# Attention on one Trainium2 core: score matmuls of a pair of heads in five runs, the last 64 keys over 128 rows, and row sums without VectorE

## The chip, the cores and the metric

The kernel runs on one core of a Trainium2 chip (trn2). The time is that of the device in microseconds (us), the median of three runs. Five engines work side by side: TensorE (PE in the profile; PEld is its weight load), VectorE (DVE), ScalarE (ACT), GpSimd (POOL) and SyncE (SP), which issues the transfers. Matmuls write PSUM, which VectorE and ScalarE read and empty into SBUF.

## The reference

Three layers follow each other; the change touches the first alone.

```python
def _attn_ref(q, k, v, f):                       # (4, 8, 576, 64), f (4, 8, 576)
    scores = scale * np.matmul(q, k.transpose(0, 1, 3, 2))
    cum = np.cumsum(np.log(np.clip(f, 0.0001, 1.0)), axis=-1)
    decay = cum[:, :, :, None] - cum[:, :, None, :]
    scores = np.where(causal, -1000000000.0, scores + decay)
    attn = np.exp(scores - np.max(scores, axis=-1, keepdims=True))
    attn = attn / (np.sum(attn, axis=-1, keepdims=True) + 1e-09)
    return np.matmul(attn, v)

def reference(...):
    x = _attn_ref(...)            # to (2304, 512)
    x = _moe_ref(x, ...)          # soft mixture of 8 experts, 4 slots each
    return _moe2_ref(x, ...)      # 4 dense experts
```

## The kernel before

**Pairs and steps.** The 32 heads are worked in 16 pairs (`pr`), four to a batch. The 576 queries of a head are cut into row blocks of 128, 128, 128, 128 and 64, and by causality row block `j` meets the first 128 (j + 1) keys (576 for the last). A pair has seven steps, each a row block of one head, and they run one after the other through all pairs as a counter `g`:

```python
STEPS = ((0, 1), (0, 3), (0, 2), (0, 4), (1, 1), (1, 3), (1, 2))   # (head of the pair, row block)
```

This document calls them step 0 to step 6. Steps 0 and 4 take row blocks 1 and 0 together (256 and 128 keys), steps 1 and 5 row block 3 (512 keys), steps 2 and 6 row block 2 (384 keys). Step 3 takes the last 64 rows of both heads at once, one head in PSUM rows 0 to 63 and one in 64 to 127, over 576 keys, in two PSUM tiles.

**What happens to a step.** `scores` makes the score matmuls of the step, in float32r, each product in two parts (L227 over 128 rows, L228 over 66; L212 for step 3). `soft` lets VectorE add the mask and take the row extreme (L198, into `p_j`), and ScalarE the exponential with its row sum (L202). Two steps later `transposes` turns `p_j` on TensorE (L261; L252 for row blocks 0 and 1) into one of two PSUM buffers of the tag `pt`, and a copy takes it to SBUF: to `pta` or `ptb` on VectorE (L170) or ScalarE (L168). The transposes of step 3 are copied half by ScalarE and half by VectorE ("the half copies", 128x256 elements each); those of steps 1 and 5 whole by VectorE (128x512), those of steps 2 and 6 by ScalarE (128x384). At step 4 the block of the last 64 rows against the last 64 keys is turned too (L254), and VectorE copies 64 rows of it into `ptb` for each head (L258).

**Products with the values.** A step behind a pair's last, `av_a` (L291) and `av_b` (L279) multiply `pta` and `ptb` with the values in plain float32, the two heads side by side as 64 columns of the array each. `av_b` comes in two stretches: key blocks 3, 4 and 0 ahead of the transposes of the next pair's step 0, and the rest of 0, 1 and 2 after its step 3 scores. Key block 4, the last 64 keys, uses 64 rows of weights where all others use 128. The values of that block lie in a tile of 128 rows whose upper 64 are zeros, and the columns of `p_4` behind 576 are set to zero once, at the start.

**Normalization and logits.** `rs` holds the row sums by row block and head. `nat` turns the pair's output back (L306) and VectorE scales it with the inverse sums (L312); `plog` makes the logits of the next layer (L325, L327) and VectorE multiplies them (L329), followed by a small one (L340) and by the copies of step 4's transposes.

**What sets the order.** TensorE runs in the order in which the code is written: in the loop over `g` first `scores(g)`, then the value products, then `transposes(g - 2)`, then `nat` and the logits. The order on VectorE, ScalarE, GpSimd and SP is made by the scheduler, and each of them works through its queue in order. Score tiles have four PSUM buffers. Steps 1 and 5 use the same `p_3`, so step 1's mask may be written only after the transposes of the pair before have read it.

Of the kernel before, what the change touches and what calls it, by code (L numbers as in the profile page):

```python
# [9 lines left out]
F32 = mybir.dt.float32  # L10
# [24 lines left out]
def soft_moe_kernel(tc, a, out):  # L35
    nc = tc.nc
    pe, dve, act, pool, sp = nc.tensor, nc.vector, nc.scalar, nc.gpsimd, nc.sync
# [10 lines left out]
    with ExitStack() as top:  # L48
# [42 lines left out]
        sm = pool_on(top, "right", "sm", 4)  # L91
# [109 lines left out]
            p = pt_in[j][:, 0:k0]  # L201
            act.activation(p, p, AF.Exp, bias=nm, scale=-1.0, accum_out=sums)  # L202

        def scores(g):
            pr, st = divmod(g, NS)
            hh, j = STEPS[st]
            h = 2 * pr + hh
            if j == 4:
                ts = [scq.tile([128, 512], F32, tag="sc", name=f"sc_{g}_{i}")[:, 0:384 - 192 * i] for i in range(2)]
                for t, k0, k1 in zip(ts, (0, 384), (384, 576)):  # L210
                    for q, k, kk, j, hx in ((qa, ka, 128, 0, 1), (qa, ka, 128, 0, 0), (qb, kb, 66, 1, 0), (qb, kb, 66, 1, 1)):
                        pe.matmul(t if hx else t[0:64], lhsT=qpad[j][0:kk] if hx else q[0][0:kk, 512:576],  # L212
                                  rhs=k[hx][0:kk, k0:k1], start=j == 0 and hx == 1,
                                  stop=j == 1 and hx == 1)
                r4 = sm.tile([128, 1], F32, tag="r4", bufs=1, name=f"r4_{pr}")
                soft(g, 4, ts, r4)
                for x in range(2):
                    i = (2 * pr + x) % 6
                    dve.tensor_copy(rs[0:64, 4, i:i + 1], r4[64 * x:64 * x + 64])
                return  # L220
            t, off = scq.tile([128, 512], F32, tag="sc", name=f"sc_{g}"), 0
            todo = []
            for c in (j,) if j > 1 else (1, 0):
                s0, n = START[c], START[c] + 128
                o = t[:, off:off + n]
                qs = slice(s0 + 64 * hh, n + 64 * hh)
                pe.matmul(o, lhsT=qa[hh][:, qs], rhs=ka[hh][:, 0:n], start=True, stop=False)  # L227
                pe.matmul(o, lhsT=qb[hh][0:66, qs], rhs=kb[hh][0:66, 0:n], start=False, stop=True)  # L228
                off += n
                todo.append((c, o))  # L230
            for c, o in todo:
                soft(g, c, (o,), rs[:, c, h % 6:h % 6 + 1])

        pta, ptb, cur = {}, {}, {}

# [3 lines left out]
        def transposes(g):  # L239
            pr, st = divmod(g, NS)  # L240
            hh, j = STEPS[st]
            h = 2 * pr + hh
            if g == NG - 1:
                t = scq.tile([128, 512], F32, tag="sc", name="pt_l").rearrange("p (i q) -> p i q", q=128)
            else:
                t = ptq.tile([128, 4, 128], F32, tag="pt", name=f"pt_{g}")
            if st in (1, 3):
                ptb[h + (st == 3)] = ptp.tile([128, 1280], F32, tag="ptb", bufs=2, name=f"ptb_{g}")
            if j == 1:
                pta[h] = ptp.tile([128, 384], F32, tag="pta", bufs=2, name=f"pta_{g}")  # L250
                for x, (c, i) in enumerate(((0, 0), (1, 0), (1, 1))):
                    pe.transpose(t[:, x, :], pt_in[c][:, 128 * i:128 * i + 128], ident)  # L252
                if st == 4:
                    pe.transpose(t[:, 3, :], pt_in[4][:, 512:640], ident)  # L254
                copy(act if g == NG - 3 else EV[1], pta[h], t[:, 0:3, :].rearrange("p a b -> p (a b)"))
                if st == 4:
                    for x in range(2):
                        dve.tensor_copy(ptb[h - 1 + x][0:64, 960:1024], t[0:64, 3, 64 * x:64 * x + 64])  # L258
                return
            for i in range(min(j + 1, 4)):  # L260
                pe.transpose(t[:, i, :], pt_in[j][:, 128 * i:128 * i + 128], ident)  # L261
            if j == 4:
                for x in range(2):
                    copy(EV[x + 4], blocks(ptb[h + x], 4)[:, :, 256:320], t[:, :, 64 * x:64 * x + 64])
                return
            c0 = 128 * (j - 2)
            copy(EV[j], blocks(ptb[h], j + 1)[:, :, c0:c0 + 128], t[:, 0:j + 1, :])
# [4 lines left out]
        def av_b(pr, i, q0, q1=320):  # L272
            if i == 3:
                av[pr] = tlq.tile([128, 512], F32, tag="av", name=f"avb_{pr}")
            t = av[pr]
            kk = 64 if i == 4 else 128
            b0 = 960 if i == 4 else 320 * i + q0
            for hh in range(2):
                pe.matmul(t[64 * hh:64 * hh + 64, q0:q1], lhsT=v_raw[pr][:kk, i, 64 * hh:64 * hh + 64],  # L279
                          rhs=ptb[2 * pr + hh][:kk, b0:b0 + q1 - q0], start=i == 3, stop=i == 2, skip_group_check=True)  # L280
            if i == 2:
                copy(EV[7], ot[pr][:, 256:576], t[:, 0:320])
                if pr + 1 < B * NP:
                    load_v(pr + 1)
# [179 lines left out]
                    csoft2(b)  # L464

        NG = NS * B * NP
        LAG = 2
        PS, PO = (3, 1)
        SPL = (3, 6)
# [25 lines left out]
        order = ExitStack()  # L495
        for g in range(NG + 4):
            pr, st = divmod(g, NS)
            if g < NG:
                scores(g)
                if g == GD:  # L500
                    for i in range(2):
                        decay(kb[i][96:128], slice(32 * i, 32 * i + 32))
                    first.close()
                    order.enter_context(tc.manual_schedule(engines={E.PE}))
                for h, s0 in ((1, 0),) if pr == 0 and st < 2 else ((2 * pr + 2, SPL[0]), (2 * pr + 3, SPL[1]), (2 * pr + 1, SPL[1] - 7)):
                    if h >= B * H:
                        continue
                    if st == s0:
                        split_a(h)
                        if 1 < h and h % 2 and h // 2 + 1 < B * NP:  # L510
                            load_q(h // 2 + 1)
                    if st == s0 + 1:
                        split_b(h)
                        if h + 2 < B * H:
                            load_k(h + 2)
                if pre and g >= GW and g % PS == PO:
                    pl = pre.pop(0)
                    if pl == "ring":
                        if not rt:
                            rt.append(ring.tile([128, 4096], F32, tag="w", name="ring_0"))  # L520
                        pl = rt[0][:, 4096 - 1024 * (len(pre) - NB + 1):4096 - 1024 * (len(pre) - NB)]
                    load_w(pl)
# [6 lines left out]
            before_tr(g - LAG + 2)  # L529
            if LAG <= g < NG + LAG:  # L530
                transposes(g - LAG)
            after_tr(g - LAG + 2)
        order.close()
        avs.close()
# [701 lines left out]
```

## Time and profile before

| what | us |
|---|---|
| median of three runs (675.5 to 676.67) | 676.22 |
| the profiled execution, its own time | 674.97 |
| its span, first to last instruction | 673.2 |
| TensorE busy in the span | 659.2 (98%) |
| VectorE busy | 493.3 (73%) |
| GpSimd busy | 419.4 (62%) |
| ScalarE busy | 342.6 (51%) |

A busy time is the union of an engine's instruction records. Matmuls are pipelined and their recorded ends are modelled, so a high share for TensorE is not TensorE at its peak, and a wait can lie under a record. The attention stage takes the first third of the span.

### The profile page before, as it was taken

Reading aid. Unit: us, or ns where it says so; the run is one execution under the profiler, and the core shown is the slowest. Engines: PE = TensorE matmul, PEld = TensorE weight load, DVE = VectorE, ACT = ScalarE, POOL = GpSimd, SP = SyncE. Lnnn points to the kernel's source line nnn. Section 1 sums busy time; section 2 is a strip of 40 time slices with the busy share of each in tenths; the row PEclk is TensorE's granted clock in tenths of the full one; section 3 lists DMA queues with packets and bytes.
Section 4 is the critical chain, followed back from the end, with each engine's and each line's share of the span. In section 5 each row is a group of like instructions: output and inputs, shape, how many; then the busy total and the mean of one; then the engine's idle time right before and its main releaser. Section 6 shows DMA issues by size and latency. Waiting matters only on the chain.

```text
span 673.2 us, 15292 instructions
## 1 busy us (share of the span) xinstructions
PE 659.2 (98%) x5634; PEld 581.6 (86%) x5634; DVE 493.3 (73%) x1358; ACT 342.6 (51%) x818; POOL 419.4 (62%) x392
## 2 busy tenths in 40 slices
PE   6999999999999998999999999999999999999997
PEld 4777777777777446999999999999999999999997
DVE  7888988988986004966778876778876767877774
ACT  5767767767764105543446443446443456543441
POOL 6667767767751046944589844589844589935443
PEclk7999999999999899999999999999999999999999
DMA  6587788733318893033000303000303000011111
GB/s 191 189 265 241 249 257 260 235 92 112 92 56 342 321 418 146 2 126 126 1 1 2 127 1 126 1 1 2 125 2 115 11 1 1 32 39 58 48 48 63
DMA packets 27138, 76.15 MB, mean 113 GB/s; under 512 B 3772, under 2 KB 4156, under 8 KB 27064
## 3 DMA queue, kind: packets, MB, share of 16 engines
q1 hardware_dynamic: 27064, 75.18, 32.5%
q8 instruction: 45, 0.74, 0.4%
q14 instruction: 29, 0.24, 0.1%
HBM read 70.31 MB, written 4.72 MB: 111 GB/s over the span
## 4 chain that ended last, share of the span: by engine, by line
PE 91%; DVE 4%; issue 2%; ACT 1%; DMA 0%; POOL 0%; DVEq 0%; ACTq 0%
PE R L1026 27%; PE Q L1026 13%; PE P L1026 6%; PE avb L279 6%; PE pt L261 6%; PE two L838 5%; PE d L1046 3%; PE sc L228 3%; PE sc L227 3%; PE sc L212 3%; PE pl L327 2%; PE two L734 2%; PE pt L252 2%; PE ava L291 2%; PE so_ps L758 2%
## 5 line engine op out<-in xcount | busy, mean ns | idle before, releaser
L904 POOL TENSOR_TENSOR s<-S,s 128x512 fp32r<-128x512 f32 x136 | 174.7, 1318 | 135.0 <-ACT s L900 135.0
L900 ACT CAST s<-S 128x512 fp32r<-128x512 f32 x136 | 75.0, 619 | 85.9 <-DVE S L896 55.0
L202 ACT ACTIVATE p<-p,nm 128x256 f32<-128x256 f32 (+2 forms) x144 | 83.4, 580 | 37.9 <-DVE nm L198 37.3
L1026 PE MATMUL R<-wh_T,s 128*128 128x256 f32 x544 | 86.6, 281 | 0.7 <-DVE acc L1009 0.7
L1009 DVE SCALAR_TENSOR_TENSOR acc<-R,dpn,acc 128x256 f32<-128x256 f32 x115 | 55.4, 482 | 37.5 <-PE R L1026 34.6
L870 ACT ACTIVATE a<-two 128x256 f32<-128x256 f32 x68 | 26.1, 383 | 96.9 <-PE two L838 96.5
L1026 PEld LDWEIGHTS R<-wh_T,s 128*128 128x128 f32 x544 | 73.5, 188 | 1.3 <-ACT a L879 1.2
L198 DVE CUSTOM_DVE_ANT_0 p<-sc,maskb 128x256 f32<-128x256 f32 (+2 forms) x144 | 66.2, 488 | 3.9 <-PE sc L212 0.9
L896 DVE SCALAR_TENSOR_TENSOR S<-two,S 128x256 f32<-128x256 f32 x136 | 57.0, 419 | 3.3 <-POOL s L904 0.9
L896 DVE SCALAR_TENSOR_TENSOR S<-two,a 128x256 f32<-128x256 f32 x136 | 56.2, 413 | 0.0
L179 POOL TENSOR_TENSOR opd<-raw,opd 64x576 fp32r<-64x576 f32 x30 | 44.3, 1477 | 11.1 <-ACT opd L168 9.8
L227 PE MATMUL sc<-opd 128*128 128x256 f32 (+3 forms) x128 | 47.4, 381 | 1.7 <-POOL opd L179 1.7
L261 PE MATMUL pt<-ident,p 128*128 128x128 f32 x285 | 47.3, 285 | 1.1 <-DVE ptb L170 0.3
L190 POOL TENSOR_TENSOR opd<-raw,opd 64x576 fp32r<-64x576 f32 x31 | 44.1, 1422 | 6.7 <-DVE opd L170 5.7
L838 PE MATMUL two<-c4t,gs 128*128 128x256 f32 x288 | 46.2, 283 | 0.3 <-ACT gs L168 0.3
L261 PEld LDWEIGHTS pt<-ident,p 128*128 128x128 f32 x285 | 31.4, 144 | 17.2 <-issue 14.6
L886 DVE SCALAR_TENSOR_TENSOR q<-two,q 128x512 fp32r<-128x512 f32 x68 | 46.2, 679 | 0.0
L1026 PE MATMUL R<-wh_T,q 128*128 128x256 f32 x272 | 43.8, 283 | 0.0
L279 PE MATMUL avb<-ptb,v 128*64 128x192 f32 (+3 forms) x384 | 43.8, 347 | 0.0
L180 POOL TENSOR_SCALAR opd<-raw 64x576 fp32r<-64x576 f32 x30 | 21.5, 717 | 35.2 <-PE sc L212 17.7
L1026 PE MATMUL Q<-wh_B,s 128*128 128x256 f32 x272 | 43.3, 281 | 0.0
L1026 PE MATMUL R<-wh_B,a 128*128 128x256 f32 x272 | 43.1, 280 | 0.0
(254 smaller groups left out, 1686.8 us busy)
## 6 DMA issues: line engine op xcount, KB each, us to landing
w<-in_w SPq DMA_DIRECT2D x50, 512.0 KB, 5.3
ring<-in_m SPq DMA_DIRECT2D x28, 512.0 KB, 6.6
raw<-in_k SPq DMA_DIRECT2D x64, 144.0 KB, 2.8
v<-in_v SPq DMA_DIRECT2D x16, 320.0 KB, 4.1
out<-acc SPq DMA_DIRECT2D x18, 256.0 KB, 2.0
raw<-in_q SPq DMA_DIRECT2D x15, 288.0 KB, 4.2
ring<-in_w SPq DMA_DIRECT2D x8, 512.0 KB, 4.5
w_opd<-in_w SPq DMA_DIRECT2D x4, 512.0 KB, 5.3
```

The lines of the kernel that those rows point to most:

```text
L198: dve.tensor_tensor_reduce(out=pt_in[j][:, k0:k0 + n], in0=sc, in1=maskb[:, m0:m0 + n], scale=-SCALE, scalar=nm, op0=ALU.add, op1=ALU.min, ...
L202: act.activation(p, p, AF.Exp, bias=nm, scale=-1.0, accum_out=sums)
L227: pe.matmul(o, lhsT=qa[hh][:, qs], rhs=ka[hh][:, 0:n], start=True, stop=False)
L261: pe.transpose(t[:, i, :], pt_in[j][:, 128 * i:128 * i + 128], ident)
L279: pe.matmul(t[64 * hh:64 * hh + 64, q0:q1], lhsT=v_raw[pr][:kk, i, 64 * hh:64 * hh + 64], rhs=ptb[2 * pr + hh][:kk, b0:b0 + q1 - q0], star ...
L838: pe.matmul(t[:, j, k], lhsT=gs[e][:, 128 * fc:128 * fc + 128], rhs=c4t[:, nb * BLK:nb * BLK + BLK])
L886: dve.scalar_tensor_tensor(o[:, 1], i, 0.0, f32(o[:, 0]), op0=ALU.max, op1=ALU.subtract)
L896: dve.scalar_tensor_tensor(sv[m, name][:, c], half[m, h][:, :, k, 128 * t:128 * t + 128], 0.0, other, op0=ALU.max, op1=op)
L900: act.copy(tile_of(m, name)[:, 0], sv[m, name])
L904: (eng or pool).tensor_tensor(o[:, 1], sv[m, name], f32(o[:, 0]), op=ALU.subtract)
L1009: dve.scalar_tensor_tensor(o, t, pcol, o, op0=ALU.mult, op1=ALU.add)
L1026: pe.matmul(t, lhsT=a[:, c, :], rhs=w[:, c, :], start=first and x == 0 and c == 0, stop=x == 2 and c == 3, skip_group_check=True)
```

## The change

The loop now takes its scores from a table: from the second pair on, the scores of step 1 are made together with those of step 0 and the scores of step 4 together with those of step 3, so that a pair has five runs of score matmuls. The mask and exponential of step 1 are held back until the transposes behind the run are written. The value products of the last 64 keys use all 128 rows, and the copies that feed them take 128 rows. The row sums of step 3 go straight into `rs` for both heads, and ScalarE copies the second head's 64 sums to the lower rows.

```diff
-        def scores(g):
+        def scores(g, hold=None):
...
-                r4 = sm.tile([128, 1], F32, tag="r4", bufs=1, name=f"r4_{pr}")
-                soft(g, 4, ts, r4)
-                for x in range(2):
-                    i = (2 * pr + x) % 6
-                    dve.tensor_copy(rs[0:64, 4, i:i + 1], r4[64 * x:64 * x + 64])
+                i, i2 = [(2 * pr + x) % 6 for x in range(2)]
+                soft(g, 4, ts, rs[:, 4, i:i + 1])
+                act.copy(rs[0:64, 4, i2:i2 + 1], rs[64:128, 4, i:i + 1])
                 return
...
             for c, o in todo:
-                soft(g, c, (o,), rs[:, c, h % 6:h % 6 + 1])
+                f = lambda c=c, o=o: soft(g, c, (o,), rs[:, c, h % 6:h % 6 + 1])
+                f() if hold is None else hold.append(f)
...
-                        dve.tensor_copy(ptb[h - 1 + x][0:64, 960:1024], t[0:64, 3, 64 * x:64 * x + 64])
+                        dve.tensor_copy(ptb[h - 1 + x][:, 960:1024], t[:, 3, 64 * x:64 * x + 64])
...
-            kk = 64 if i == 4 else 128
             b0 = 960 if i == 4 else 320 * i + q0
             for hh in range(2):
-                pe.matmul(t[64 * hh:64 * hh + 64, q0:q1], lhsT=v_raw[pr][:kk, i, 64 * hh:64 * hh + 64],
-                          rhs=ptb[2 * pr + hh][:kk, b0:b0 + q1 - q0], start=i == 3, stop=i == 2, skip_group_check=True)
+                pe.matmul(t[64 * hh:64 * hh + 64, q0:q1], lhsT=v_raw[pr][:, i, 64 * hh:64 * hh + 64],
+                          rhs=ptb[2 * pr + hh][:, b0:b0 + q1 - q0], start=i == 3, stop=i == 2, skip_group_check=True)
...
+        RUNS = {0: (0, 1), 2: (2,), 3: (3, 4), 5: (5,), 6: (6,)}
...
+            held = []
             if g < NG:
-                scores(g)
+                for x in RUNS.get(st, ()) if pr else (st,):
+                    scores(g - st + x, held if st == 0 and x else None)
...
             if LAG <= g < NG + LAG:
                 transposes(g - LAG)
+            for f in held:
+                f()
             after_tr(g - LAG + 2)
```

On TensorE, in the middle of a pair, behind the last score matmul of step 3 (`sc_1`), before:

```order
L212 MATMUL sc_1_1447<-opd_92 128x192
L279 MATMUL avb_1433<-ptb_1304,v_1301 64x128
L279 MATMUL avb_1433<-ptb_1339,v_1301 64x128
L279 MATMUL avb_1433<-ptb_1304,v_1301 64x320
L279 MATMUL avb_1433<-ptb_1339,v_1301 64x320
L279 MATMUL avb_1433<-ptb_1304,v_1301 64x320
L279 MATMUL avb_1433<-ptb_1339,v_1301 64x320
L261 MATMUL pt_1479<-ident,p_125 128x128 x4
L227 MATMUL sc_1486<-opd_92 128x256
L228 MATMUL sc_1486<-opd_92 128x256
L227 MATMUL sc_1486<-opd_92 128x128
L228 MATMUL sc_1486<-opd_92 128x128
```

and of the change:

```order
L212 MATMUL sc_1_1433<-opd_92 128x192
L225 MATMUL sc_1448<-opd_92 128x256
L226 MATMUL sc_1448<-opd_92 128x256
L225 MATMUL sc_1448<-opd_92 128x128
L226 MATMUL sc_1448<-opd_92 128x128
L277 MATMUL avb_1419<-ptb_1301,v_1298 64x128
L277 MATMUL avb_1419<-ptb_1325,v_1298 64x128
L277 MATMUL avb_1419<-ptb_1301,v_1298 64x320
L277 MATMUL avb_1419<-ptb_1325,v_1298 64x320
L277 MATMUL avb_1419<-ptb_1301,v_1298 64x320
L277 MATMUL avb_1419<-ptb_1325,v_1298 64x320
L260 MATMUL pt_1474<-ident,p_125 128x128 x4
```

The four score matmuls of step 4 moved ahead of the second stretch of value products and of the transposes of step 1.

On ScalarE, at the same place of the pair, from the exponential of step 3 (`p_126`) to that of step 5 (`p_125`); `p_123` and `p_122` are step 4's, `ot` the copy of the products. Before:

```order
L202 ACTIVATE p_126,r_7_1456<-p_126,nm_4_1_1459 128x576
L168 COPY ot<-avb_1433 128x320
L168 COPY ptb_1480<-pt_1501 128x3x128
L202 ACTIVATE p_123,rs<-p_123,nm_1_0_1491 128x256
L202 ACTIVATE p_122,rs<-p_122,nm_0_0_1494 128x128
L202 ACTIVATE p_125,rs<-p_125,nm_3_0_1509 128x512
L168 COPY ptb_1480<-pt_1512 128x4x64
```

and of the change:

```order
L202 ACTIVATE p_126,rs<-p_126,nm_4_1_1444 128x576
L202 ACTIVATE p_123,rs<-p_123,nm_1_0_1453 128x256
L217 COPY rs<-rs 64x1
L202 ACTIVATE p_122,rs<-p_122,nm_0_0_1456 128x128
L168 COPY ot<-avb_1419 128x320
L168 COPY ptb_1475<-pt_1485 128x3x128
L168 COPY ptb_1475<-pt_1496 128x4x64
L202 ACTIVATE p_125,rs<-p_125,nm_3_0_1493 128x512
```

Step 4's exponentials and the row-sum copy moved ahead of the three copies, and the half copy (128x4x64) ahead of step 5's exponential.

On VectorE, from there to the logit multiplication (`pln`); the rows L198 without an input read out a reduction. Before (the two row-sum copies of L219 stand right ahead of these rows):

```order
L170 COPY ptb_1480<-pt_1479 128x4x128
L198 ISA p_123,nm_1_0_1491<-sc_1486,maskb 128x256
L198 ISA nm_1_0_1491 128x1
L198 ISA p_122,nm_0_0_1494<-sc_1486,maskb 128x128
L198 ISA nm_0_0_1494 128x1
L198 ISA p_125,nm_3_0_1509<-sc_1506,maskb 128x512
L198 ISA nm_3_0_1509 128x1
L312 TENSOR_TENSOR xn_1182<-nat_1520,ri_1430 128x4x128
L198 ISA p_124,nm_2_0_1529<-sc_1526,maskb 128x384
L198 ISA nm_2_0_1529 128x1
L170 COPY ptb_1513<-pt_1512 128x4x64
L329 TENSOR_TENSOR pln_1546<-pl_1539,ri_1430 128x320
```

and of the change:

```order
L198 ISA p_123,nm_1_0_1453<-sc_1448,maskb 128x256
L198 ISA nm_1_0_1453 128x1
L198 ISA p_122,nm_0_0_1456<-sc_1448,maskb 128x128
L198 ISA nm_0_0_1456 128x1
L170 COPY ptb_1475<-pt_1474 128x4x128
L198 ISA p_125,nm_3_0_1493<-sc_1490,maskb 128x512
L198 ISA nm_3_0_1493 128x1
L170 COPY ptb_1497<-pt_1496 128x4x64
L310 TENSOR_TENSOR xn_1170<-nat_1504,ri_1416 128x4x128
L198 ISA p_124,nm_2_0_1513<-sc_1510,maskb 128x384
L198 ISA nm_2_0_1513 128x1
L327 TENSOR_TENSOR pln_1530<-pl_1523,ri_1416 128x320
```

Step 4's reductions moved ahead of the copy of step 1's transposes, and the half copy ahead of the normalization (`xn`) and of step 6's reduction (`p_124`).

## Rows read from the trace of the kernel before

**Rows 1.** Windows of two pairs: length; PE, PEld, DVE, ACT, POOL busy; clock; DMA.

```profile
109.08:120.72 11.64, 11.64 (x98) 9.16 (x97) 10.02 (x38) 8.39 (x26) 8.34 (x9) 1.00 0.75 237
147.14:159.05 11.91, 11.83 (x97) 9.17 (x97) 10.29 (x38) 8.42 (x26) 8.41 (x9) 1.00 0.35 105
```

**Rows 2.** TensorE's timeline in a pair: start us, length us, line, tiles, count.

```profile
147.84 1.23 PE L279 MATMUL avb<-ptb,v 128*64 128x192 f32 x12
149.01 0.55 PE L252 MATMUL pt<-ident,p 128*128 128x128 f32 x3
...
150.58 1.52 PE L279 MATMUL avb<-ptb,v 128*64 128x128 f32 x12
152.02 0.66 PE L261 MATMUL pt<-ident,p 128*128 128x128 f32 x4
...
153.52 0.39 PE L228 MATMUL sc<-opd 66*128 66x512 f32 x1
153.99 0.63 PE L261 MATMUL pt<-ident,p 128*128 128x128 f32 x4
```

**Rows 3.** VectorE's timeline in the same pair.

```profile
152.93 0.31 DVE L219 COPY rs<-r 64x1 f32<-64x1 f32 x2 [0.99 <-ACT p L202]
153.16 0.68 DVE L170 COPY ptb<-pt 128x512 f32<-128x512 f32 x1
...
155.09 0.69 DVE L312 TENSOR_TENSOR xn<-nat,ri 128x512 f32<-128x512 f32 x1
155.70 0.55 DVE L198 CUSTOM_DVE_ANT_0 p<-sc,maskb 128x384 f32<-128x384 f32 x1
...
156.32 0.42 DVE L170 COPY ptb<-pt 128x256 f32<-128x256 f32 x1
156.69 0.49 DVE L329 TENSOR_TENSOR pln<-pl,ri 128x320 f32<-128x320 f32 x1
...
157.76 0.33 DVE L258 COPY ptb<-pt 64x64 f32<-64x64 f32 x2
```

**Rows 4.** TensorE's timeline, the end of that pair.

```profile
157.10 0.23 PE L227 MATMUL sc<-opd 128*128 128x128 f32 x1
157.16 0.27 PE L228 MATMUL sc<-opd 66*128 66x128 f32 x1
157.28 0.62 PE L261 MATMUL pt<-ident,p 128*128 128x128 f32 x4
...
157.97 0.40 PE L228 MATMUL sc<-opd 66*128 66x512 f32 x1
158.25 0.52 PE L261 MATMUL pt<-ident,p 128*128 128x128 f32 x3
...
159.75 0.50 PE L279 MATMUL avb<-ptb,v 128*64 128x192 f32 x4
```

**Rows 5.** VectorE's timeline, the end of that pair.

```profile
158.95 0.67 DVE L170 COPY ptb<-pt 128x512 f32<-128x512 f32 x1
```

**Rows 6.** Weight loads over fifteen pairs, by form: busy us, mean ns | idle before.

```profile
L279 PEld LDWEIGHTS avb<-ptb,v 64*64 64x64 f32 x60 | 2.9, 131 | 4.2 <-issue 4.2
```

**Rows 7.** ScalarE's timeline in the same pair.

```profile
152.03 0.78 ACT L202 ACTIVATE p<-p,nm 128x576 f32<-128x576 f32 x1 [0.83 <-DVE nm L198]
...
152.81 0.41 ACT L168 COPY ot<-avb 128x320 f32<-128x320 f32 x1
153.54 0.48 ACT L168 COPY ptb<-pt 128x384 f32<-128x384 f32 x1 [0.33 <-PE pt L261]
154.34 0.51 ACT L202 ACTIVATE p<-p,nm 128x256 f32<-128x256 f32 x1 [0.32 <-DVE nm L198]
...
154.85 0.39 ACT L202 ACTIVATE p<-p,nm 128x128 f32<-128x128 f32 x1
...
155.94 0.35 ACT L168 COPY ptb<-pt 128x256 f32<-128x256 f32 x1
```

**Rows 8.** ScalarE's groups by line, the attention stage, its smallest operation.

```profile
L385 ACT ACTIVATE al<-mm,dm 128x1 f32<-128x1 f32 x3 | 0.9, 292 | 0.0
```

## Prediction, made before the change was run

> **What bounds the kernel now.** I first read the windows view, one window for each pair of heads in the attention stage, since every line of the change lies there. In a usual pair TensorE is busy for 11.83 of 11.91 us at a granted clock of 1.00, VectorE for 10.29, ScalarE for 8.42 and GpSimd for 8.41 [rows 1]. Twelve of the fifteen pairs whose runs are joined look like this; three, one behind each of the first three batches, are longer by that batch's own work on TensorE. So the stage goes at TensorE's pace. But its busy time hides waits, since a matmul's record runs on while the next one is held, so I read starts, not lengths, from its timeline.
>
> Three waits show there. First, the 512-column matmul at 153.52 is followed by the transposes of step 3 only at 153.99, 0.47 us later [rows 2]; an equal one later in the pair needs 0.28 (157.97 to 158.25) [rows 4], so 0.19 is lost. The transposes want one of two PSUM buffers, which VectorE empties with the copy at 153.16 (0.68 us) [rows 3]. That copy is late because VectorE stood idle for 0.99 us before the two row-sum copies of L219, which wait for ScalarE's exponential [rows 3]. Ten pairs show a loss like this (one of them half of it); in two, as in the 11.64 us pair [rows 1], it is absent.
>
> Second, near the end of the pair TensorE and VectorE arrive together. VectorE's two small copies end at 157.76 + 0.33 = 158.09 [rows 3], and the transposes that reuse their PSUM buffer start at 158.25 [rows 4]. The four-block copy at 158.95 ends at 159.62 [rows 5], and the value products that read it start at 159.75 [rows 4]. 0.15 us from the end of such a copy to TensorE's start is also what the first wait shows (153.84 to 153.99) [rows 2, 3], so VectorE, from the logit multiplication (156.69) [rows 3] on, is as much the bound here as TensorE.
>
> Third, the loads of 64-row weights for the last 64 keys were preceded by 4.2 us of idle time in fifteen pairs, 0.28 each [rows 6], with no other engine named.
>
> **The products over 128 rows.** The first stretch of value products runs from 147.84 to 149.01, 1.17 us for 192 + 64 + 192 = 448 columns a head; the second from 150.58 to 152.02, 1.44 us for 128 + 320 + 320 = 768 columns [rows 2]. At the second one's rate the first would take 1.44 x 448 / 768 = 0.84, so the detour into 64 rows and back costs 0.33 us. The idle time before the 64-row loads alone is 0.28 [rows 6], as the lower of two readings; nothing shows a 64-column product in the 128-row form. If it took as long as the next larger one there, 128 columns, it would cost 64 x 1.44 / 768 = 0.12 us more, and the gain would be 0.16 to 0.21. I take 0.30, between the two readings and without the floor, since the 64-column products that are there already leave no room for one: 0.28 of the 0.33 is the idle time before them. All 16 pairs have this once: 16 x 0.30 = 4.8 us, between 2.6 and 5.3. Behind the stretch TensorE goes on with transposes whose inputs are long ready, and with the scores of step 3. The VectorE copies from 64 to 128 rows keep their 64 columns and their time.
>
> **The joined score runs.** Leaving a score run for transposes costs 0.12 us after a 128-column matmul (157.16 to 157.28) against 0.06 to the next matmul inside the run (157.10 to 157.16) [rows 4]. So each join frees about 0.06 us, two in a pair, 15 x 0.12 = 1.8 us, if nothing waits. At the pair's start (step 1 with step 0) I take nothing: the same transposes still need the two small copies and the value products still need the four-block copy, and VectorE's order from the logit multiplication to both is unchanged, so TensorE only waits where it worked. At step 3 the value products and the transposes of step 1 move behind step 4's scores, about 0.4 us later, and with them VectorE's 0.68 us copy, so the 0.19 us loss stays although L219 is gone.
>
> The Trainium skill, TensorEngine Tiling (Array Packing), Key Properties, says that changing the tiling mode drains TensorE, while changing the tile within a mode does not. By that rule the joins would free nothing, since scores and transposes both use the whole array, and only the 64-row detour would gain; the 0.06 us above are a cost that the rule does not have. The sum is the same by either, because I count the joins at nothing.
>
> **The row sums, and the new order on ScalarE and VectorE.** VectorE loses two copies (0.31 us) and their 0.99 us wait [rows 3]. But softmax of step 4 now comes earlier on ScalarE, ahead of its PSUM copies. I follow its queue in the usual pair. The exponential of step 3 starts at 152.03 as before, and the next operation can start at 152.81 [rows 7]. Before, from there: product copy, block copy at 153.54, step 4's exponentials, step 5's, half copy at 155.94 to 156.29 [rows 7]. Now: exponential 0.51, row-sum copy, exponential 0.39, product copy 0.41, block copy 0.48, half copy 0.35 [rows 7]. For the row-sum copy I take 0.25: the smallest ScalarE operation here takes 0.29 with an exponential [rows 8]. The sum is 2.39, so the half copy ends at 155.20, 1.1 us earlier. The Trainium skill, ScalarE: Activation LUTs, Rules for kernel authors, budgets about 0.3 us for an ACTIVATE, which would add 0.05.
>
> On VectorE the matching half copy (156.32 now, 0.03 after ScalarE's ended [rows 3, 7]) moves ahead of the normalization at 155.09 and of step 6's reduction at 155.70. It would run from 155.23; 0.37 later (156.32 to 156.69) comes the normalization, which ran at 155.09 before, 0.61 later the reduction, and after its 0.55 the logit multiplication: 155.23 + 0.37 + 0.61 + 0.55 = 156.76, against 156.69 before [rows 3]. So what waits behind the half copy on VectorE is late, and the earlier ScalarE copy nearly pays it: I charge 0.04, as operations there start some hundredths before the one ahead ends (155.70 against 155.09 + 0.69) [rows 3]; in ten usual pairs that is 0.4 us. In the two pairs without the 0.19 loss TensorE was that much ahead, so these lose about 0.2 each, 0.4 us. The three long pairs have other TensorE work between; I count nothing there. Bounds: if the chain is 0.1 shorter, TensorE sets the time and 1 us comes back; if the row-sum copy takes twice as long, 12 x 0.25 = 3 us more.
>
> **Sum.** 4.8 - 0.4 - 0.4 = 4.0 us. The profiled execution took 674.97 us (span 673.2 and 1.77 around it), so 671.0 for one like it; it lay 1.25 us under the median of 676.22, so **672.2** beside that median. Its own range is 670.9 to 673.8.
>
> **The rivals.**
> *The waits go too.* If the four-block copy and ScalarE's chain are earlier than I work out, the 0.19 and the joins are gained: 10 x 0.19 + 1.8 + 0.8 = 4.5 us more, 667.7. For it: VectorE's 0.99 us idle time vanishes. Against: the ties at 158.25 and 159.75 [rows 4]. 0.15.
> *A smaller share of the detour.* The 64-column step has a floor, or the loss moves to the next VectorE copy: 16 x 0.16 to 0.21 less the 0.8, so a gain of 1.8 to 2.6, about 674. 0.15.
> *The change doesn't do what it says.* The gap before the 64-row loads comes from something else that stays, such as the wait for the value weights; then only the charges of 0.8 us are left against the long pairs' joins of 3 x 0.12: about 676.6. 0.10.
> *Slower: ScalarE's queue becomes the bound.* The row-sum copy reads another partition half of what the exponential's accumulator just wrote, and stands ahead of four operations on which VectorE's half copy, the normalization and the logits depend. From 0.25 + 4.0 / 12 = 0.58 us for it on, the gain is gone; at 0.8 us it is 12 x 0.22 = 2.6 us slower, 678.8. Against: no ScalarE operation as small as this takes that long [rows 8]. 0.08.
> The forecast keeps 0.52.
>
> **How the numbers follow.** A median of this kernel can tell about 0.2%, 1.35 us. The forecast, the first rival and the smaller share (0.52, 0.15 and most of 0.15) are faster than 674.87; the no-effect case and the rest are within; the ScalarE case is slower: 0.79, 0.13, 0.08. The range 668.3 to 675.0 holds the forecast, the smaller share, and the nearer half of the first rival.
>
> **What the profile after would show.** No 64-row weight loads and a first stretch of products of about 0.87 us show the first step right. Transposes of step 3 still about 0.47 us behind their 512-column matmul show that the copy holds them; 0.28 would show the first rival. The logit multiplication 4.6 to 4.8 us after step 3's exponential (152.03 to 156.69 now) [rows 3, 7] shows ScalarE's chain sized right; later than that, the last rival. Usual pairs should take about 11.65 us. The prediction is wrong if VectorE's chain from the logits to the value products gets shorter or longer, which I hold fixed.

## The result, and the profile after

The changed kernel takes 681.44 us (median of five runs, 679.45 to 683.12) against 676.22 for the kernel before: 1.0073 times as long, 95% interval 1.0048 to 1.0099. The forecast was 672.2, faster. The sign was wrong. The ratios of all runs here leave out two executions far above the rest, 713.19 us in e1 and 2203.93 us in e7, which the medians include.

The profiled execution has a span of 681.3 us, 8.1 more than before. It was the slowest of the five (683.12 us), and the one of the kernel before lay under its median, so the losses below are larger than the 5.2 us between the medians. To see where, I took the start of each pair's first value products (`ava`, L291 before, L289 after) from TensorE's timeline; the distance from one to the next is a "stretch", 15 in all, and stretch n runs from pair n - 1 to pair n (pairs 0 to 15).

| stretches | before, us | after, us | sum of the differences |
|---|---|---|---|
| 1, 2, 4, 11, 12 (usual) | 11.87 to 11.93 | 11.55 to 11.66 | -1.5 |
| 3, 7, 8 | 11.80, 11.90, 11.64 | 14.13, 12.65, 13.30 | +4.7 |
| 5, 9, 13 (with a batch's end, long) | 14.52 | 14.55, 14.29, 14.51 | -0.2 |
| 6, 10, 14 (behind it) | 11.89 to 11.90 | 12.86, 12.86, 12.87 | +2.9 |
| 15 (the last) | 10.29 | 11.23 | +0.9 |
| ahead of the first `ava`, behind the last | 23.26 and 465.5 | 24.00 and 466.1 | +1.3 |

So 8.5 us were lost in seven stretches, and the usual ones gained about 0.3 each, as forecast. The last row holds a difference of the clock: over the 24.75 us behind the last `ava` TensorE's granted clock was 0.93 before and 0.86 after. The windows view shows four of them (one late, one behind a batch's end, one usual, the last); it answers to [rows 1]:

```profile
47.14:61.27 14.13, 11.85 (x97) 9.28 (x96) 10.98 (x39) 9.22 (x29) 9.27 (x10) 1.00 0.74 223
87.48:100.34 12.86, 11.74 (x97) 9.33 (x96) 10.75 (x38) 8.63 (x27) 8.53 (x9) 1.00 0.74 249
153.44:165.04 11.60, 11.52 (x97) 9.29 (x96) 10.07 (x36) 8.54 (x27) 8.35 (x9) 1.00 0.36 107
204.02:215.25 11.23, 10.42 (x90) 8.21 (x89) 8.93 (x31) 7.09 (x23) 3.21 (x6) 1.00 0.70 264
```

TensorE is busy for 11.85 of 14.13 us in the late stretch and for 11.52 of 11.60 in the usual one, at the same granted clock: it waits. The view of waits names for what (us in total, times, longest), over the whole attention stage:

```profile
PE avb L277 <- DVE xn L338: 3.1, 3, 1.1
PE ava L289 <- DMA v<-in_v: 2.4, 3, 1.1
PE pt L251 <- ACT p L202: 1.4, 2, 0.9
PE nat L304 <- ACT ot L168: 1.3, 2, 0.7
PE pt L260 <- ACT p L202: 1.0, 2, 0.5
PE pt_l L260 <- ACT p L202: 0.7, 1, 0.7
```

None of these stood in the profile before. Each has a place of its own.

**The usual stretch came out as worked out.** TensorE's timeline from 153.44, which answers to [rows 2]:

```profile
153.44 0.87 PE L289 MATMUL ava<-pta,v 128*64 128x256 f32 x8
154.15 0.94 PE L277 MATMUL avb<-ptb,v 128*64 128x192 f32 x12
155.01 0.55 PE L251 MATMUL pt<-ident,p 128*128 128x128 f32 x3
...
159.51 0.40 PE L226 MATMUL sc<-opd 66*128 66x512 f32 x1
159.99 0.63 PE L260 MATMUL pt<-ident,p 128*128 128x128 f32 x4
```

The first stretch of products takes 0.86 us (154.15 to 155.01) for 1.17 before, and the transposes of step 3 are still 0.48 behind their matmul. ScalarE's queue, which answers to [rows 7]:

```profile
157.97 0.78 ACT L202 ACTIVATE p<-p,nm 128x576 f32<-128x576 f32 x1 [0.77 <-DVE nm L198]
...
159.15 0.19 ACT L202 ACTIVATION_READ_ACCUMULATOR p<-p,nm 128x1 f32 x1
159.36 0.19 ACT L217 COPY rs<-rs 64x1 f32<-64x1 f32 x1
159.58 0.40 ACT L202 ACTIVATE p<-p,nm 128x128 f32<-128x128 f32 x1
```

The row-sum copy takes the queue from 159.34 to 159.58, 0.24 us.

**The late stretches: the value load.** SyncE's queue in a usual stretch, first before, then after (start, length of the issue with its wait, line, tiles, count; `L133` is the value load of the next pair, `L128` half a key load). In the kernel before the stretch began at 147.14, in the changed one at 153.44:

```profile
151.63 0.47 SPq L128 DMA_DIRECT2D raw<-in_k  x1
152.20 0.54 SPq L133 DMA_DIRECT2D v<-in_v  x1
154.38 0.48 SPq L128 DMA_DIRECT2D raw<-in_k  x1
```

```profile
157.64 3.22 SPq L128 DMA_DIRECT2D raw<-in_k  x2
160.95 0.54 SPq L133 DMA_DIRECT2D v<-in_v  x1
161.58 0.63 SPq L185 DMA_DIRECT2D opd<-opd  x1
```

Before, the value load stood between the two key halves and started 5.1 us into the stretch, 6.85 ahead of the products that read it (159.05). After, it stands behind both, the second of which waits for GpSimd to finish with the buffer (2.2 us here), and starts 7.5 us into the stretch, 4.1 ahead of 165.04. Over stretches 1 to 12 it is 5.0 to 6.2 us into the stretch before and 7.5 to 10.2 after. In stretch 3 it comes too late; SyncE's queue, then TensorE:

```profile
48.90 1.13 SPq L128 DMA_DIRECT2D raw<-in_k  x2
...
56.31 0.49 SPq L128 DMA_DIRECT2D raw<-in_k  x1
57.33 1.03 SPq L133 DMA_DIRECT2D v<-in_v  x1
```

```profile
59.80 0.33 PE L226 MATMUL sc<-opd 66*128 66x384 f32 x1
61.27 0.87 PE L289 MATMUL ava<-pta,v 128*64 128x256 f32 x8 [1.15 <-DMA v<-in_v]
```

Its start at 57.33 is late for another transfer too: ScalarE's cast of the next query rows, ahead of step 3's exponential in its queue, had waited for them:

```profile
49.08 0.60 ACT L202 ACTIVATE p<-p,nm 128x384 f32<-128x384 f32 x1
...
52.59 0.67 ACT L168 CAST opd<-raw 64x576 fp32r<-64x576 f32 x1 [2.81 <-DMA raw<-in_q]
53.17 0.77 ACT L202 ACTIVATE p<-p,nm 128x576 f32<-128x576 f32 x1
```

That query load took 6.3 us from issue to landing; its counterpart before took 4.2. In the changed kernel the value load was issued 3.2 us ahead of it (43.05 and 46.27), before 6.3 us ahead (40.24 and 46.53).

**Behind a batch's end.** VectorE at the start of stretch 6, before:

```profile
84.66 0.47 DVE L329 TENSOR_TENSOR pln<-pl,ri 128x320 f32<-128x320 f32 x1
85.06 0.27 DVE L340 TENSOR_TENSOR xn<-pl,ri 64x128 f32<-64x128 f32 x1
85.25 0.67 DVE L198 CUSTOM_DVE_ANT_0 p<-sc,maskb 128x512 f32<-128x512 f32 x1
```

and VectorE and TensorE there in the changed kernel:

```profile
87.97 0.67 DVE L198 CUSTOM_DVE_ANT_0 p<-sc,maskb 128x512 f32<-128x512 f32 x1
...
88.58 0.48 DVE L327 TENSOR_TENSOR pln<-pl,ri 128x320 f32<-128x320 f32 x1
88.98 0.27 DVE L338 TENSOR_TENSOR xn<-pl,ri 64x128 f32<-64x128 f32 x1
```

```profile
87.48 0.87 PE L289 MATMUL ava<-pta,v 128*64 128x256 f32 x8
89.40 0.99 PE L277 MATMUL avb<-ptb,v 128*64 128x192 f32 x12 [1.05 <-DVE xn L338]
```

At the start of these three pairs TensorE also makes the logit products of the batch's last pair. Joined, step 1's scores stand ahead of them, and the held reduction of step 1 (87.97) stands ahead of the logit multiplication (88.58), where before it stood behind it (84.66, then 85.25). `avb` takes the PSUM buffer that the small operation behind it frees (88.98 + 0.27), and waits 1.05 us.

**The last stretch.** The last pair's turned row blocks of step 6 wait 0.74 us for their exponential, which stands behind a ScalarE copy of step 4's transposes (213.63) that itself waits for TensorE:

```profile
213.63 0.48 ACT L168 COPY pta<-pt 128x384 f32<-128x384 f32 x1 [1.32 <-PE pt L253]
214.01 0.62 ACT L202 ACTIVATE p<-p,nm 128x384 f32<-128x384 f32 x1
```

### The profile page after: what moved, and what is told of

It is laid out like the page before. It is cut to its first block, busy times and chain, and to the rows that moved or that the text cites. A ratio compares the mean times of both kernels' runs of the same rounds, so it can differ in the third digit from the quotient of the medians.

```text
span 681.3 us, 15207 instructions
## 1 busy us (share of the span) xinstructions
PE 657.1 (96%) x5634; PEld 582.2 (85%) x5634; DVE 494.5 (73%) x1326; ACT 344.7 (51%) x834; POOL 417.2 (61%) x392
## 3 DMA queue, kind: packets, MB, share of 16 engines
HBM read 70.31 MB, written 4.72 MB: 110 GB/s over the span
## 4 chain that ended last, share of the span: by engine, by line
PE 77%; DVE 7%; ACT 6%; DMA 5%; issue 3%; POOL 1%; SPq 1%; ACTq 0%; DVEq 0%; POOLq 0%
PE R L1029 26%; PE Q L1029 13%; PE P L1029 6%; PE two L841 5%; PE avb L277 3%; PE d L1049 3%; PE pt L260 3%; DMA raw<-in_q 3%; ACT p L202 2%; PE two L737 2%; PE sc L212 2%; PE so_ps L761 2%; PE sc L225 1%; PE sc L226 1%; PE pt L251 1%
## 5 line engine op out<-in xcount | busy, mean ns | idle before, releaser
L198 DVE CUSTOM_DVE_ANT_0 p<-sc,maskb 128x256 f32<-128x256 f32 (+2 forms) x144 | 67.2, 488 | 4.9 <-PE sc L212 1.8
L225 PE MATMUL sc<-opd 128*128 128x256 f32 (+3 forms) x128 | 45.0, 367 | 1.6 <-POOL opd L179 1.6
L260 PE MATMUL pt<-ident,p 128*128 128x128 f32 x285 | 42.1, 281 | 1.8 <-ACT p L202 1.0
L1029 PE MATMUL Q<-wh_T,s 128*128 128x256 f32 x272 | 43.0, 280 | 0.0
L1029 PE MATMUL R<-wl_T,s 128*128 128x256 f32 x272 | 43.0, 280 | 0.0
```

Of the source, the lines that this page charges most:

```text
L198: dve.tensor_tensor_reduce(out=pt_in[j][:, k0:k0 + n], in0=sc, in1=maskb[:, m0:m0 + n], scale=-SCALE, scalar=nm, op0=ALU.add, op1=ALU.min, ...
L1029: pe.matmul(t, lhsT=a[:, c, :], rhs=w[:, c, :], start=first and x == 0 and c == 0, stop=x == 2 and c == 3, skip_group_check=True)
```

## The experiments

My theory from the traces: the parts gain what was forecast; the joins lose it, in the pairs behind a batch's end and the last one, and by moving the value load in SyncE's queue. Rivals: the pace alone makes loads late, whatever their order; ScalarE's row-sum copy is the cost; weight loads crowd the transfers. Ratios are to the kernel before, run in the same group, with 95% intervals.

### Parts alone and joins one at a time

e1 keeps of the change only the products over 128 rows, e2 these and the row sums. e3 and e4 are the changed kernel with one join less:

```diff
 RUNS (e3)
-        RUNS = {0: (0, 1), 2: (2,), 3: (3, 4), 5: (5,), 6: (6,)}
+        RUNS = {0: (0, 1), 2: (2,), 3: (3,), 4: (4,), 5: (5,), 6: (6,)}
 RUNS (e4)
-        RUNS = {0: (0, 1), 2: (2,), 3: (3, 4), 5: (5,), 6: (6,)}
+        RUNS = {0: (0,), 1: (1,), 2: (2,), 3: (3, 4), 5: (5,), 6: (6,)}
```

> The kernel before with the 128-row products of the last 64 keys alone; scores in seven runs, row sums on VectorE. SyncE's queue of transfers stands in the same order as before. Theory (the products gain what was predicted, and the changed kernel lost it again because the load of the next pair's values now stands behind a load of keys in SyncE's queue): about 0.30 us less in each of 16 pairs, 671 to 672 us, values never late. Rival (a faster pace alone makes the loads late, whatever their order): pairs of 11.6 us with waits for loads between them, 675 to 681 us.

> The 128-row products and the row sums on ScalarE, scores in seven runs. SyncE's queue: the values still ahead of the keys or between their two halves as before, some weight loads moved by one place. Theory (order of the value load in SyncE's queue): no late values, 670 to 673 us. Rival 1 (pace alone): 675 to 681 us. Rival 2 (row-sum copy on ScalarE is the cost): slower than the kernel with the 128-row products alone by 2 us or more.

> The changed kernel with steps 3 and 4 of a pair apart again (the join at the pair's start stays). The value products of step 3 stand ahead of step 4's scores as before, and in SyncE's queue the value load is again ahead of the keys or between their halves. Theory (the join at step 3 moved the value load behind the keys in that queue): the loss is gone, 668 to 673 us. Rival (pace alone, or the join at the start): 677 us or more.

> The changed kernel with steps 0 and 1 of a pair apart again (the join of steps 3 and 4 stays). In SyncE's queue the value load stands behind both halves of the keys in the later pairs, as in the changed kernel. Theory: the loss stays, 678 to 682 us, with TensorE's value products waiting for the value load in the pairs behind a batch's end. Rival (the join at the start is the cause): 668 to 673 us.

| run | us | ratio (interval) | usual stretches | 6, 10, 14 | 15 |
|---|---|---|---|---|---|
| e1 | 671.75 | 0.9949 (0.9922 to 0.9975) | 11.59, some 11.36 | 11.58 | 10.02 |
| e2 | 672.20 | 0.9958 (0.9936 to 0.9979) | 11.35 | 11.5 to 11.7 | 10.02 |
| e3 | 673.95 | 0.9976 (0.9958 to 0.9995) | 11.36 | 12.63 | 10.50 |
| e4 | 677.26 | 1.0023 (1.0002 to 1.0043) | 11.60 | 11.96 | 11.22 |

The products over 128 rows are worth their gain, without late loads. The row sums add nothing to it: e2's usual stretches fall to 11.35, but its later two long ones take 15.12 and 14.81 where e1's take 14.46 and 14.45, and its ratio is no better than e1's. Each join costs: the one at the start in the stretches behind a batch's end, the one at step 3 in the usual stretches (0.25) and in the last. The value load is issued 4.7 to 6.6 us into stretches 1 to 12 in e1 and e2, which have no stretch late by the value load, and 7.5 to 8.8 us in e4, where 2, 3, 4 and 8 took 11.8 to 12.5. In e3 it is issued after 4.7 to 6.2, but for two stretches: in 8, which took 14.13, ScalarE's cast waited 3.29 us for the query rows, and the value load, behind a key half, went out after 10.2 us (the 8.8 in 9 fell into a long one). The rival that blames the ScalarE copy falls with e2, and the rival that blames the pace alone as well: at 11.35 us e2 is faster in its usual stretches than e4, and none of them is late by a load. e3 came out 1.0 us above its range, e4 0.7 under its own.

### The logit multiplication first, and the order of the transfers

e5 writes the held reductions behind the logits of a batch's last pair. e6 takes the changed kernel with SyncE's queue in program order, which puts the value load ahead of both key halves in every pair; e7 is e6 with the value load behind them; e8 is the kernel before with the order of e6:

```diff
 e5
+            after_tr(g - LAG + 2)
             for f in held:
                 f()
-            after_tr(g - LAG + 2)
 e6, e7, e8
-                    order.enter_context(tc.manual_schedule(engines={E.PE}))
+                    order.enter_context(tc.manual_schedule(engines={E.PE, E.SP}))
 e7, besides
-                    load_v(pr + 1)
+                    late_v.append(pr + 1)
...
+                if st == 4 and late_v:
+                    load_v(late_v.pop())
```

> The changed kernel, but in the pairs behind a batch's end the logit multiplication of the last pair stands ahead of step 1's held reduction on VectorE's queue again, as in the kernel before; TensorE's order is that of the changed kernel. Theory: those three pairs take 12.86 us in the changed kernel against 11.60 for the usual ones because the value products wait for a PSUM buffer that this multiplication frees; with it first 3 x 1.26 = 3.8 us go, 677 to 678 us, and the rest of the loss (pairs 3, 6, 7 and 8, which wait for loads) stays. Rival (late value loads hold those pairs too): 681 us, no change.

> The changed kernel with SyncE's queue in program order: the value load ahead of both key halves in every pair, the weight loads spread over more pairs. Theory (the scheduler's new order of that queue holds pairs 3, 6, 7 and 8, which lose 2.5, 1.1, 1.1 and 1.7 us against 11.60): about 6 us less, 674 to 677 us; the three pairs behind a batch's end keep their 1.26 us. Rival (the pace alone makes loads late, or the queue's order is not the cause): 680 us or more.

> The same as the run with SyncE in program order, but each value load stands behind both halves of the key load of its step. Theory (a value load behind a key load is late, since the key load waits for GpSimd): 2 to 6 us more than that run, with value products waiting for the value load. Rival (the place of the value load does not matter, only the crowding with weight loads): the same as that run within 1 us.

> The kernel before, with SyncE's queue in the same program order as in the run of the changed kernel: what the change does when both have one order of transfers. Theory: this order by itself is worth little to the kernel before, which has no late loads: 674 to 678 us. Rival (this order frees transfers for any kernel): 670 us or less.

| run | us | ratio (interval) | stretches 1 to 4, 7, 8 | 6, 10, 14 | 15 |
|---|---|---|---|---|---|
| e5 | 678.33 | 1.0034 (1.0013 to 1.0054) | 11.55 to 13.1 | 12.25, 12.44, 12.26 | 11.23 |
| e6 | 677.48 | 1.0011 (0.9989 to 1.0033) | 11.55 to 11.61 | 12.86 to 12.87 | 11.23 |
| e7 | 680.54 | 1.0059 (1.0033 to 1.0086) | 11.6 to 12.8 | 12.87 to 13.07 | 11.23 |
| e8 | 676.00 | 0.9997 (0.9976 to 1.0018) | 11.88 to 12.2 | 11.89 to 11.91 | 10.32 |

e6 against e7 differs in the place of the value load alone, and that is worth 3.1 us. In e6 every late stretch is gone, and no matmul waits for a transfer in the attention stage (two weight loads do, 0.5 us in all); this is everything that the view of waits lists for the matmuls:

```profile
PE avb L277 <- DVE xn L338: 3.1, 3, 1.1
PE pt_l L260 <- ACT p L202: 0.7, 1, 0.7
PE pt L260 <- DVE ptb L170: 0.4, 1, 0.4
```

In e7 the first row of that view is again the value load:

```profile
PE ava L289 <- DMA v<-in_v: 3.5, 4, 1.1
```

e5 was half right: the wait of the value products falls from 1.05 to 0.4 us at the longest, but the stretches keep 12.25 to 12.44, since TensorE's own order still has the logit products late. Its median fell by more than those three stretches give (1.6 us); late loads vary from run to run. e8 shows that the order of e6 by itself gains nothing (0.9997). It even has a stretch late by the value load, 4 (12.22): the load went out at 64.54, and the products that waited for it began at 71.34, 6.8 us later. e5 and e6 ended 0.3 and 0.5 us above their ranges.

### Transfers in one order, parts and joins apart

e9 is e2, e10 is e3, each with the order of transfers of e6. e11 has the row sums alone, e12 is e6 with the joins left out where they hurt:

```diff
 e12
-                for x in RUNS.get(st, ()) if pr else (st,):
+                apart = not pr or st in (0, 1) and pr in (6, 10, 14) or st in (3, 4) and pr == B * NP - 1
+                for x in (st,) if apart else RUNS.get(st, ()):
```

> 128-row products and row sums on ScalarE, scores in seven runs, SyncE's queue in program order (as in the runs e6 and e8). Theory (the two other parts gain, the joins take it back): usual pairs of 11.35 us against 11.91, no late loads, 12 us-pairs behind a batch's end gone: 11 x 0.55 + 0.5 = 6.5 us less than the kernel before in that order, 669 to 671 us. Rival (the row sums on ScalarE earn nothing beside the products): 671.5 to 673 us.

> The run e9 with the join of steps 0 and 1 added. Theory (that join moves the logit products of a batch's last pair closer to the value products that reuse their PSUM buffer): usual pairs stay at 11.35 us, the three pairs behind a batch's end take 12.6 us against 11.6: about 3 us more than e9, 672 to 674 us. Rival (the join is worth 0.06 us a pair or nothing): e9's time within 0.7 us.

> The kernel before with the row sums of the last rows on ScalarE alone: no 128-row products, no joins. Theory (VectorE's wait of 0.99 us goes and with it TensorE's 0.19 in ten pairs): about 2 us less, 673 to 675 us, transposes of step 3 at 0.28 us behind their 512-column matmul. Rival (the prediction's slower case: the copy on ScalarE costs 0.58 us or more and delays its queue): 676 us or more.

> The run e6 with the runs of steps 0 and 1 apart in the three pairs whose start holds the logit products of a batch's last pair (6, 10 and 14 of 0 to 15), and those of steps 3 and 4 apart in the last pair; joined elsewhere. Theory: the three pairs of 12.87 us come down to 12.0, the last stretch of 11.23 to about 10.3: 3.5 us less than e6, 673 to 675 us. Rival (those stretches are long for another reason): e6's 677.5 us within 1.

| run | us | ratio (interval) | usual stretches | 6, 10, 14 | 15 |
|---|---|---|---|---|---|
| e9 | 673.55 | 0.9967 (0.9947 to 0.9987) | 11.35; 12.6 to 13.2 in 4, 7, 8 | 11.70 | 10.05 |
| e10 | 675.13 | 0.9991 (0.9973 to 1.0009) | 11.35; 12.1 and 11.9 in 4, 7 | 12.62 | 10.04 |
| e11 | 676.99 | 1.0028 (1.0007 to 1.0048) | 11.63 | 12.00 | 10.31 |
| e12 | 673.00 | 0.9965 (0.9953 to 0.9977) | 11.60 | 11.96 | 10.02 |

By ratios e12 is 0.46%, 3.1 us, faster than e6 (3.5 expected): those stretches are the joins' doing. e10 ended 1.1 us above its range, with the 12.62 that its theory gave. e9 missed its 669 to 671: in stretches 4 and 7 the value products waited for their load again, although in 7 it stood first and went out 6.3 us into the stretch, 7.0 ahead of the products that it then held:

```profile
PE ava L288 <- DMA v<-in_v: 3.0, 2, 1.8
```

That the faster pace made this load slow is not shown: it took 7.0 us to land, and the one in e8 took 6.8 at 11.90 us a pair in the same order of transfers. The time left for it changes little, from 6.9 us in e8's usual stretches to 6.4 to 6.7 in e9's.

Stretch 8 of e9 (12.93) is long for another reason: its value load is not late, but TensorE runs slower behind the wait. TensorE's timeline, then the window of the products:

```profile
110.62 1.12 PE L288 MATMUL ava<-pta,v 128*64 128x256 f32 x8 [1.80 <-DMA v<-in_v]
111.52 1.71 PE L276 MATMUL avb<-ptb,v 128*64 128x192 f32 x12
```

```profile
111.52:113.72 2.20, 2.20 (x19) 1.50 (x16) 0.50 (x2) 0.00 (x0) 0.00 (x0) 0.50 0.91 263
```

After the 1.80 us in which TensorE stood idle its granted clock was 0.50, the 1.2 GHz level, and the twelve products took 1.71 us where they take 0.94 at 1.00 a pair earlier. No other run here has the lower level between its first and last `ava`.

e11 was a miss: alone, the row sums on ScalarE cost 0.28%. The usual stretches gained their 0.27 us, but the long ones took 16.28, 14.88 and 14.89 for 14.52. The last section shows one operation in them that grew and a wait behind it; in the first of them ScalarE's cast also waited 3.1 us for the query rows, and TensorE 0.6 for the ScalarE operation behind that cast and 0.7 for `s_sb` (see there). That ScalarE's copy is not it is argued, not shown: the usual stretches hold the same copy and are shorter.

### Without the weight loads, and the free joins

e13 is e7 with the 33 weight loads moved behind the attention loop (so the rest of the kernel waits for them). e14 is e3 with steps 0 and 1 apart in pairs 6, 10 and 14, and e15 is e14 with the order of e6.

> The run e7 (value loads behind both key halves, SyncE in program order) with the weight loads of the later stage issued only behind the attention loop. The whole gets longer, since those weights then come late; what counts are the pairs. Theory (a late place in the queue costs only where the queue and the transfers are crowded with weight loads): pairs 2, 4, 7 and 8, which took 12.4, 12.5, 12.8 and 12.5 us in e7, come down to 11.6; the three behind a batch's end stay at 12.87 and the last stretch at 11.2. Rival (the place behind the keys alone makes the values late): those pairs stay above 12.2 us.

> The run e3 (128-row products, row sums on ScalarE, steps 0 and 1 joined, steps 3 and 4 not) with steps 0 and 1 apart in pairs 6, 10 and 14; SyncE's queue as the scheduler makes it. Theory: those three pairs come from 12.63 down to 11.6, 3 us less than e3's 673.95: 670 to 672 us, faster than the kernel before and no slower than the 128-row products alone (671.75). Rival (loads are late at the pace of 11.35 us): 673 to 675 us.

> The run e14 with SyncE's queue in program order. Theory: the same pairs as in e14, 670 to 673 us. Rival (at 11.35 us a pair the loads of pairs 4, 7 and 8 are late in this order, as in e9): 673 to 675 us.

e13 (one execution) kept its late stretches: 12.45, 12.34, 12.27 and 12.87 us in 2, 3, 7 and 8. My theory that the weights have to crowd the queue fell; the place behind the keys is enough, as its rival said. Two stretches of e13 in the windows view, one late, one not, with the same small traffic (last two columns: share of the DMA engines' time, GB/s):

```profile
48.44:60.78 12.34, 11.59 (x97) 9.28 (x98) 10.06 (x36) 8.52 (x25) 8.24 (x9) 1.00 0.41 117
152.17:163.82 11.65, 11.57 (x99) 9.29 (x98) 10.12 (x36) 8.60 (x27) 8.39 (x9) 1.00 0.36 107
```

Both had the value load issued 8.1 to 8.2 us into the stretch; in the first it took 4.1 us to land, in the second 3.5. A load issued 3.5 us ahead of its use is late or in time by the spread of its landing alone.

e14: 672.04 us, 0.9951 (0.9926 to 0.9976), stretches 6, 10 and 14 down to 11.71, no late stretch. e15: 672.36, 0.9959 (0.9937 to 0.9982), two stretches of 11.9. Both beat the two kernels, and neither beats e1.

## Why the prediction was wrong

**Right: the usual pair.** The products over 128 rows took 0.31 us off their stretch (1.17 to 0.86; 0.30 forecast). In e1 the usual stretches and those behind a batch's end gained 0.3 each, but the three long ones only 0.07 (why was not tested); so the term of 4.8 us measured 3.5 (0.51% by the ratio). The transposes of step 3 stayed 0.48 us late, the logit multiplication came 4.72 us after step 3's exponential (4.6 to 4.8 forecast), the usual pair took 11.60 (11.65 forecast), and the row-sum copy cost 0.24 (0.25 forecast; the 0.3 quoted beside it is a budget for an operation that reads its bias from an operand, which this copy does not).

**The step that failed first: "At the pair's start (step 1 with step 0) I take nothing."** Its reason was that "VectorE's order from the logit multiplication to both is unchanged". That was read from the usual pair. In pairs 6, 10 and 14 the multiplication belongs to the batch's last pair and stands at the pair's start, and there the held reduction went ahead of it: 3 x 0.97 = 2.9 us lost. VectorE's chain from the logits to the value products, which the prediction said it held fixed, got longer there. "The three long pairs have other TensorE work between; I count nothing there" looked at the long stretches and not at the ones behind them. The join at step 3 was taken to leave the 0.19 us loss in place, which is so (11.35 without it, 11.60 with it), but the 10.29 us last stretch, which has no next pair to cover it, was not worked out: +0.9. All joins together cost e6 against e9 0.44%, 3.0 us, and e9's own late stretches (4.7 us above 11.35 in its trace) hide a part of their cost.

**The step that was missing: SyncE's queue.** The text moved the second stretch of value products behind step 4's scores and followed what VectorE copies next, but not that those products also free the buffer into which the next values are loaded, and that the scheduler would then queue that load behind the keys. No rival named a transfer. By ratios, the order of the transfers is worth 0.62%, 4.2 us (changed kernel to e6), and a load's place alone 0.48%, 3.2 us (e6 to e7).

**The sum set right.** From the forecast (0.9941) to the result (1.0073) it is 1.32%, 8.9 us. The four terms above add up to 9.3: 2.9 behind the batches' ends, 0.9 in the last stretch, 4.2 for the order of the transfers and 1.3 that the products over 128 rows fell short of. They come from traces and ratios of different runs, so they agree with it only roughly. The slower rival had the right sign by the wrong way: the row-sum copy is cheap.

**Open:** why one value load takes 3.0 and another 4.1 us to land in e13, and one in e9 7. Of stretches 3, 7 and 8 in the changed kernel, 7 is late by the value load's wait (1.0 of the 1.05 us above a usual one). In 3 and 8 (2.5 and 1.7 above) that wait is 1.1 and 1.0, and TensorE also waits 0.7 and 0.5 us for ScalarE behind the late cast; why the query load took 6.3 us is not shown.

## What to carry to other kernels

When an edit moves the last reader of a buffer, follow the load that fills this buffer next: where it now stands in the issuing queue, what the entry ahead of it waits for, and how much time is left to its first use. Work the sum out for every kind of stretch (usual, long, behind the long one, last), not for the usual one times its number. Here the part worth keeping was the one that changed no order: the 128-row products alone, 0.5% faster.

## Hardware behaviour that I had not expected

One VectorE operation of 128x160 elements with two inputs in SBUF (`cn`, L366 before) took 0.31, 0.76 or 1.5 us, by when a GpSimd operation on SBUF ran. VectorE in e14, then GpSimd:

```profile
177.73 1.52 DVE L364 TENSOR_TENSOR cn<-ce,cs 128x160 f32<-128x160 f32 x1
179.18 0.73 DVE L416 SCALAR_TENSOR_TENSOR s_sb<-s_sb,al,sa 128x512 f32<-128x512 f32 x1
```

```profile
177.65 1.42 POOL L179 TENSOR_TENSOR opd<-raw,opd 64x576 fp32r<-64x576 f32 x1
```

And in e1, where VectorE came first:

```profile
176.75 0.31 DVE L365 TENSOR_TENSOR cn<-ce,cs 128x160 f32<-128x160 f32 x1
```

```profile
176.83 1.51 POOL L179 TENSOR_TENSOR opd<-raw,opd 64x576 fp32r<-64x576 f32 x1
```

Started 0.08 us behind the GpSimd operation, VectorE's ended 0.18 behind its end; in the changed kernel it started 0.84 behind, took 0.76 and ended 0.19 behind. Started 0.08 ahead, VectorE's took 0.31, and GpSimd's 1.51 for 1.42. The Trainium skill, SBUF — State Buffer, Who interferes with whom, says that a VectorE operation with two SBUF inputs contends with a GpSimd operation that reads SBUF, and that the order of issue decides who blocks; these rows agree with it, though GpSimd lost only 0.09 us while 0.23 of VectorE's operation was left.

What this costs the kernel is shown only in part. In the three long stretches `cn` takes 0.31 in the kernel before and in e1, 0.76 in the changed kernel, and 1.47 to 1.52 in e9, e11 and e14. Behind it on VectorE stands `s_sb` (179.18 above). In e9, e11, e12 and e14 TensorE's weight loads for the logits wait for `s_sb`, 1.2 to 1.7 us over the three long stretches, which take 14.6 to 14.9 there (one 16.28); in the kernel before, in e1 and in the changed kernel none waits, and they take 14.3 to 14.6. The length of `cn` alone does not decide it: it takes 1.5 in e3 and e10 too, whose long stretches are 14.3 to 14.5, and 0.76 in e12.
